# Batch 0's first quarter of q through the hardware DMA queue, and batch 6's softmax sums by matmul

## The chip, the core and the metric

The kernel runs on one core of a Trainium2 chip. The metric is the device time of one launch, in microseconds (us); smaller is better. Engines are named as the profile names them: PE (TensorE, matmuls; PEld its weight loads), DVE (VectorE), ACT (ScalarE), POOL (GpSimd) and SP (SyncE). A DMA that SP issues goes through the hardware queue (q1, `hardware_dynamic`), one that POOL issues through the software queue (q0, `software_dynamic`).

## The reference

A Linformer attention, in which keys and values are projected from 1024 positions to 64 by E and F, and then a feed-forward layer whose hidden layer is the maximum of three projections. There are 8 batches, 8 heads of width 64, and 1024 positions.

```python
def _attn_ref(q, k, v, E, F):
    k_proj = np.einsum('ks,bhsd->bhkd', E, k)
    v_proj = np.einsum('ks,bhsd->bhkd', F, v)
    scale = 1.0 / np.sqrt(q.shape[-1])
    scores = scale * np.matmul(q, k_proj.transpose(0, 1, 3, 2))
    scores = scores - np.max(scores, axis=-1, keepdims=True)
    attn = np.exp(scores)
    attn = attn / (np.sum(attn, axis=-1, keepdims=True) + 1e-09)
    return np.matmul(attn, v_proj).astype(np.float32)

def _moe_ref(x, w1, w2, w3, w_out):
    h = np.maximum(np.maximum(x @ w1, x @ w2), x @ w3)
    return (h @ w_out).astype(np.float32)

# x is the attention's output, as (8192 tokens, 512); w1, w2, w3 are (512, 768), w_out is (768, 512)
```

## The kernel before

The kernel writes its own order for every engine. PE is kept on the feed-forward layer of batch b, and the attention of batch b + 1 is put in between. Inputs are cast to bf16 on their way in by POOL's DMAs; E and F come as fp32 through SP's queue and are cast on DVE and ACT. This is the order of the first loads:

```python
nc.sync.dma_start(out=ef_f[0:KP], in_=E)
nc.sync.dma_start(out=ef_f[KP:P], in_=F)
# load_q, load_kv, load_w: nc.gpsimd.dma_start, fp32 in DRAM to bf16 in SBUF
load_q(LO, slice(0, SPC))        # heads 0 to 3, 4 of 8 rows of each partition: a quarter of q
load_kv(1, LO)                   # k, heads 0 to 3
load_q(HI, slice(0, SPC))
load_kv(1, HI)
load_kv(2, slice(0, 2))          # v, two heads
load_kv(2, slice(2, 4))
# ... identity and constants, weights, the rest of v and q
```

At the start, E and F are turned into `efT`, q's first quarter is turned into `qT`, and k of heads 0 to 3 is projected. The `idle` matmuls compute nothing that is used; they keep PE running.

```python
def turn_ef():
    for i in range(2):
        cols = slice(i * S // 2, (i + 1) * S // 2)
        copy("vs"[i], ef_b[:, cols], ef_f[:, cols])     # fp32 to bf16, on DVE and ACT
    # ... eight 128x128 transposes of ef_b on PE
    for i in range(2):
        copy("vs"[i], efT[:, 4 * i:4 * i + 4, 0:P], ...)

def q_duo(u):                     # per head: 64-wide transposes, 16 of them
    t, ns = bank()
    t = t.bitcast(BF16)
    for gg in range(2):
        heads_q(0, 2 * u + gg, range(SPC), t[:, gg * CHUNK:(gg + 1) * CHUNK])
    o = qTs[0].rearrange("a (g si) p -> a g si p", si=SI)
    copy("v", o[:, 2 * u:2 * u + 2, 0:SPC, :], ...)

def k_duo(u):
    for si in range(SI):
        nc.tensor.matmul(
            out=t[0:KP, 0:4 * D], lhsT=efT[:, si, 0:KP],
            rhs=k_t[:, 4 * u:4 * u + 4, si, :],
            start=(si == 0), stop=(si == SI - 1),
        )
    # ... copied to kp0

idle(3, warm_f)
turn_ef()
q_duo(0)
copy("v", efT[:, :, P:P + KP], efT[:, :, KP:P])
idle(1, warm_f)
k_duo(0)
# ... turn kp0, scores, exponentials, then q_duo(1), k_duo(1), the values of batch 0
```

The first chunk's maxima go through the buffer `hs`, one 512-wide fp32 row for each of six blocks; it is first written at about 25 us.

```python
hs = ffn_sb.tile([P, NJT, CHUNK], FP32, name="hs", bufs=1)
```

There are two ways to get the softmax sums. `zc` lets PE add the exponentials with a matrix of ones and zeros (`pick`, eight matmuls), and ACT inverts the sums. The other way turns the exponentials by a DMA transpose (`turn_p`), adds them on DVE (`sum_p`) and inverts and spreads them from there (`spread_z`). The plan for the loop of batch b, which serves batch n = b + 1, from batch 4 on:

```python
out = {
    (0, 1): [sc(n, 1, now=True), sc(n, 2, now=True), sc(n, 3)],
    (0, 3): [zc(n)],
    (1, 2): [vx(n, 0), vx(n, 1)],
    (1, 6): [vx(n, 2), vx(n, 3)],
}
if n + 1 == B:                    # batch 7: turn_p, sum_p, spread_z in place of zc
    ...
if n + 1 < B:
    out[0, 4] = [qd(n + 1)]
    out[1, 2] = [kvproj(n + 1)] + out[1, 2]
    out[1, 6] += [sc(n + 1, 0)]
if n in (6,):                     # batch 6: the same, with its own places
    del out[0, 3]
    out[0, 4] = [turn_p(n, g) for g in range(NPAIR)]
    # ...
```

Of the kernel before, what the change touches and what calls it, by code (L numbers as in the profile page):

```python
# [15 lines left out]
def kernel(  # L16
# [13 lines left out]
    nc = tc.nc  # L30
# [46 lines left out]
    def two():  # L77
        n = min(range(0, 8, 2), key=lambda n: max(free[n:n + 2]))
        deal((n, n + 1))
        return psum_t[:, n:n + 2, :], (n, n + 1)  # L80
# [20 lines left out]
    def copy(eng, o, i, ns=(), dt=0.65):  # L101
        done = {  # L102
            "v": nc.vector.tensor_copy, "s": nc.scalar.copy, "g": nc.gpsimd.tensor_copy
        }[eng](out=o, in_=i)
        runs(eng, clock["pe"] if ns else 0.0, dt, ns)
        return done
# [49 lines left out]
    def load_q(heads, sis):  # L156
        nc.gpsimd.dma_start(
            out=q_t[:, heads, sis], in_=view(q, 0)[:, heads, sis]
        )
# [4 lines left out]

    LO, HI, ALL = slice(0, H // 2), slice(H // 2, H), slice(0, H)
    V2, V3 = slice(4, 6), slice(6, 8)
    load_q(LO, slice(0, SPC))
    load_kv(1, LO)
    load_q(HI, slice(0, SPC))
    load_kv(1, HI)  # L170
# [122 lines left out]
    def turn_p(b, g):  # L293

        def f():
            if b not in s_T:
                s_T[b] = att.tile([P, NPAIR, 2, SPC, 2], FP32, name="s_T")
            p_T[b, g] = att.tile([P, 2, CHUNK // 2], FP32, name="zi0", bufs=4).rearrange(  # L300
                "p a f -> p (a f)"
            ).bitcast(BF16).rearrange("p (n x) -> p n x", x=P)
            nc.sync.dma_start_transpose(
                out=p_T[b, g], in_=pTs[b, g, 0].rearrange("p h f -> p (h f)")
            )
        return f
# [43 lines left out]
    def vx(b, g):  # L350
        def f():
            scale_x(b, g, 0, SI, values(b, g, 0, SI))
        return f
# [75 lines left out]

    q_pk = {}  # L430

    def pack_q(b, gs, lo, nsi):


        def f():
            if b not in q_pk:
                q_pk[b] = att.tile([P, NPAIR, SI, 2, D], BF16, name="q_p", bufs=1)
            for g in gs:
                copy(
                    "s", q_pk[b][:, g, lo:lo + nsi].rearrange("p si h d -> p h si d"),  # L440
                    qkv[b][0][:, 2 * g:2 * g + 2, lo:lo + nsi], (), 0.58,
                )
        return f

# [184 lines left out]
    def turn_ef():  # L629
        for i in range(2):  # L630
            cols = slice(i * S // 2, (i + 1) * S // 2)
            copy("vs"[i], ef_b[:, cols], ef_f[:, cols])
        t, ns = two()
        t = t.bitcast(BF16)[:, 0]
        src = ef_b.rearrange("k (p si) -> k p si", si=SI)
        for si in range(SI):
            nc.tensor.transpose(
                out=t[:, si * P:(si + 1) * P], in_=src[:, :, si], identity=ident
            )
        pe(0.6)  # L640
        for i in range(2):
            copy(
                "vs"[i], efT[:, 4 * i:4 * i + 4, 0:P],
                t[:, i * CHUNK:(i + 1) * CHUNK].rearrange("p (si x) -> p si x", x=P), ns,
            )
# [46 lines left out]
    def q_duo(u):  # L692
# [5 lines that stand above are left out]
        copy(  # L698
            "v", o[:, 2 * u:2 * u + 2, 0:SPC, :],
            t.rearrange("a (g si p) -> a g si p", si=SPC, p=P), ns, 0.7,  # L700
        )

    C0 = (0, SPC)

    def z(g):
# [5 lines left out]
    idle(3, warm_f)  # L711
    at(6.3)
    turn_ef()
    q_duo(0)
    copy("v", efT[:, :, P:P + KP], efT[:, :, KP:P])
    idle(1, warm_f)
    at(9.0)
# [22 lines left out]
    v_pair(1)  # L740
    at(17.4)

    ffn_sb = ctx.enter_context(tc.tile_pool(name="ffn_sb", bufs=2))
    hTs = {}

    def up_mm(h, i, b, ch, jt, cts, first=0, last=NCT - 1):
# [14 lines left out]
    def up_first(work):  # L761


        def then(key):
            run_later()
            for f in work.get(key, []):
                f()

        hs = ffn_sb.tile([P, NJT, CHUNK], FP32, name="hs", bufs=1)
        hTs[0, 0] = ffn_sb.tile([P, NJT, CHUNK], BF16, name="hT")  # L770
        jts = range(NJT)
        h = {}
        for ct, js in (
            (0, range(0, 4)), (1, range(0, 4)), (0, range(4, 6)), (1, range(4, 6)),
            (2, jts), (3, jts),
        ):
            for jt in js:
                if jt not in h:
                    t, ns = two()
                    for n in (0, 1):  # L780
                        h[jt + n] = t[:, n], ns[n:n + 1]
                up_mm(h[jt][0], 0, 0, 0, jt, (ct,))
                if ct == NCT - 1:
                    copy("sv"[jt % 2], hs[:, jt], *h[jt])
                then((0, ct, jt))
        for i in (1, 2):
            h = []
            for jt in jts:
                h.append(bank())
                up_mm(h[jt][0], i, 0, 0, jt, range(NCT // 2))  # L790
                then((i, "a", jt))
            for jt in jts:
                up_mm(h[jt][0], i, 0, 0, jt, range(NCT // 2, NCT))
                most(hs[:, jt] if i == 1 else hTs[0, 0][:, jt, :], *h[jt], hs[:, jt])
                then((i, jt))
# [93 lines left out]
    def plan(b):  # L889
        n = b + 1  # L890
        if b == 0:
            return {
                (0, 6): [
                    duo[1].sums, duo[1].values, duo[0].scale, duo[1].invert,
                ],
                (0, 7): [
                    qd(1, range(2)), duo[1].scale, qd(1, range(2, 4), "s"), store_now,
                ],
                (1, 1): [kproj(1)],
                (1, 2): [kt(1)],  # L900
                (1, 3): [sc(1, 0, now=True), sc(1, 1), vproj(1), ld(2)],
                (1, 4): [za(1, 0), sc(1, 2, now=True)],
                (1, 5): [za(1, 1)],
                (1, 6): [sc(1, 3, now=True)],
                (1, 7): [za(1, 2)],
                (1, 8): [za(1, 3)],
            }
        if b == 1:
            return {
                (0, 0): [qd(2)],  # L910
                (0, 3): [kproj(2), vproj(2), ld(3, (0,))],
                (0, 4): [kt(2)],
                (0, 5): [sc(2, 0, now=True), sc(2, 1, now=True), sc(2, 2)],
                (0, 6): [sc(2, 3, now=True)],
                (0, 8): [zc(2, nc.gpsimd), ld(3, (1, 2))],
                (1, 1): [qd(3)],
                (1, 3): [vx(2, 0), vx(2, 1)],
                (1, 6): [vx(2, 2), vx(2, 3)],
            }
        if b == 2:  # L920
            return {
                (0, 2): [kproj(3), vproj(3), ld(4)],
                (0, 3): [kt(3)],
                (0, 4): [sc(3, 0, now=True), sc(3, 1)],
                (0, 5): [sc(3, 2, now=True), sc(3, 3, now=True)],
                (0, 7): [zc(3)],
                (0, 8): [qd(4)],
                (1, 3): [kproj(4), vproj(4), ld(5), vx(3, 0), vx(3, 1)],
                (1, 4): [kt(4)],
                (1, 8): [vx(3, 2), vx(3, 3), sc(4, 0)],  # L930
            }
        if n == B:
            return {}
# [6 lines that stand above are left out]
        if n + 1 == B:  # L940
            del out[0, 3]
            out[0, 2] = [turn_p(n, g) for g in range(NPAIR)]
            out[0, 8] = [sum_p(n, 0), sum_p(n, 1)]
            out[0, 9] = [sum_p(n, 2), sum_p(n, 3), spread_z(n)]
            out[1, 5] = out.pop((1, 2))
            out[1, 8] = out.pop((1, 6))
        if n + 1 < B:
            out[0, 4] = [qd(n + 1)]
            out[1, 2] = [kvproj(n + 1)] + out[1, 2]
            out[1, 6] += [sc(n + 1, 0)]  # L950
        if n in (6,):
            del out[0, 3]
            out[0, 4] = [turn_p(n, g) for g in range(NPAIR)]
            out[0, 5] = [qd(n + 1)]
            out[0, 6] = [sum_p(n, 0)]
            out[0, 7] = [sum_p(n, 1)]
            out[0, 8] = [sum_p(n, 2), sum_p(n, 3), spread_z(n)]
            out[1, 2] = [kvproj(n + 1)]
            out[1, 5] = [vx(n, 0), vx(n, 1)]
            out[1, 8] = [vx(n, 2), vx(n, 3), sc(n + 1, 0)]  # L960
            del out[1, 6]
        if n + 2 < B:
            out[1, 3] = [ld(n + 2)]
        return out
# [68 lines left out]
```

## Time and profile before

| what | value |
|---|---|
| time, median of three | 397.53 us (397.27 to 397.54) |
| span of the profiled run | 395.5 us |
| PE busy | 385.6 us, 98% |
| DVE busy | 213.1 us, 54% |
| ACT busy | 149.8 us, 38% |
| E, issue to landing | 3.7 us |
| F, issue to landing | 4.1 us |
| first matmul on k (L655) | starts at 9.90 us |
| eight selection matmuls of `zc` (L264) | 0.61 us from the first to the modelled end of the last |
| one DVE sum of the other way (L310) | 1.21 us |

A line such as `L655 PE MATMUL banks<-k_t,efT` names the source line, the engine, the operation, and what it writes and reads. Times in the timeline are from the start of the span. "Idle before" a group of instructions names what ended the wait. Packets of a DMA queue are counted for all 16 DMA engines together.

### The profile page before, as it was taken

What the parts mean: (1) busy time and instruction counts of PE and PEld (TensorE: products, weight loads), DVE (VectorE), ACT (ScalarE), POOL (GpSimd) and SP (SyncE); (2) the same over time, 40 slices, a digit from 0 to 9 for tenths busy, and PEclk for the clock granted to TensorE, in tenths of its full rate; (3) what the DMA queues carried; (4) which work ended last, traced back from release to release, by engine and by line L of the source; (5) the groups of instructions that cost most, each with busy time, mean ns of one, the idle gap of its engine ahead of it and who ended that gap; (6) DMA issues with size and microseconds to landing.
All of it is one profiled execution on the core that took longest, in us unless ns stands there. A gap on an engine that the chain in (4) does not pass through costs nothing.

```text
span 395.5 us, 5594 instructions
## 1 busy us (share of the span) xinstructions
PE 385.6 (98%) x2181; PEld 173.3 (44%) x2222; DVE 213.1 (54%) x321; ACT 149.8 (38%) x232; POOL 34.4 (9%) x49
## 2 busy tenths in 40 slices
PE   7999999999999999999999999999999999999996
PEld 3544443453445445444444444444444444444443
DVE  2348756751764525655273544744956566655251
ACT  2535638527222562263323532234322623132322
POOL 7440011000400200200002000200000000000000
PEclk9999999999999999999999999999999999999999
DMA  9999999977999999999979969599975425720202
GB/s 147 205 206 207 205 254 142 244 159 160 234 178 257 160 225 201 232 174 201 225 210 140 251 148 250 117 220 187 228 183 160 111 51 163 159 108 0 108 0 106
DMA packets 76250, 68.39 MB, mean 173 GB/s; under 512 B 40448, under 2 KB 68736, under 8 KB 76224
## 3 DMA queue, kind: packets, MB, share of 16 engines
q0 software_dynamic: 29104, 30.41, 48.2%
q1 hardware_dynamic: 46976, 37.56, 38.2%
q8 instruction: 17, 0.28, 0.3%
q10 hardware_dynamic: 144, 0.07, 0.1%
q14 instruction: 9, 0.07, 0.0%
HBM read 69.73 MB, written 16.97 MB: 219 GB/s over the span
## 4 chain that ended last, share of the span: by engine, by line
PE 92%; DVE 2%; DMA 2%; issue 1%; ACT 1%; POOL 0%; DVEq 0%; ACTq 0%; POOLq 0%
PE banks L748 61%; PE banks L856 20%; PE banks L239 2%; DMA k_t<-in_k_dram 2%; PE banks L219 2%; PE banks L412 2%; PE banks L587 1%; DVE xT L375 1%; PE banks L264 1%; ACT zi_all L364 1%; ACT zl L358 1%; PE banks L655 1%; DVE m L817 0%; DVE hT L758 0%; PE banks L626 0%
## 5 line engine op out<-in xcount | busy, mean ns | idle before, releaser
L748 PE MATMUL banks<-xT,w_sb 128*128 128x512 bf16 x1123 | 254.7, 379 | 2.0 <-DVE xT L375 0.3
L748 PEld LDWEIGHTS <-w_sb 128*128 128x128 bf16 x1152 | 110.3, 98 | 136.2 <-issue 7.2
L817 DVE TENSOR_TENSOR m<-banks,h1s 128x512 f32<-128x512 f32 x90 | 62.1, 691 | 117.6 <-ACT h1s L813 71.7
L813 ACT COPY h1s<-banks 128x512 f32<-128x512 f32 x90 | 52.7, 585 | 121.8 <-PE banks L748 121.0
L856 PE MATMUL banks<-wout_sb,hT 128*128 128x512 bf16 x367 | 85.8, 380 | 0.9 <-issue 0.3
L758 DVE TENSOR_TENSOR hT<-banks,m 128x512 bf16<-128x512 f32 x90 | 62.3, 692 | 9.3
L856 PEld LDWEIGHTS <-hT 128*128 128x128 bf16 x378 | 35.2, 98 | 48.4 <-issue 6.9
L102 ACT COPY o_sb<-banks 128x512 f32<-128x512 f32 (+2 forms) x57 | 32.9, 577 | 60.5 <-PE banks L856 57.6
L375 DVE TENSOR_TENSOR xT<-banks,zi_all 128x1024 bf16<-128x1024 f32 x28 | 33.1, 1219 | 14.8 <-PE banks L239 10.2
L230 ACT ACTIVATE pT<-banks 128x1024 bf16<-128x1024 f32 (+1 forms) x32 | 30.2, 975 | 16.0 <-PE banks L219 16.0
L201 POOL DMA_DIRECT2D q_t<-in_q_dram x7 | 6.1, 878 | 197.6 <-DVE m L817 80.9
L102 ACT CAST vp<-banks 64x256 bf16<-64x256 f32 (+1 forms) x11 | 4.7, 424 | 20.5 <-DVE kp L102 11.2
L102 DVE CAST vp<-banks 64x256 bf16<-64x256 f32 (+2 forms) x15 | 6.7, 444 | 9.8 <-ACT vp L102 7.3
L239 PE MATMUL banks<-pT,vp 64*64 64x512 bf16 (+1 forms) x128 | 10.3, 375 | 0.2 <-DVE vp L102 0.2
L102 DVE COPY q_p<-q_t 128x1024 bf16<-128x1024 bf16 x26 | 9.8, 438 | 0.0
L219 PE MATMUL banks<-qT,kpT 64*64 64x512 bf16 (+1 forms) x128 | 9.7, 372 | 0.0
L310 DVE TENSOR_REDUCE s_T<-zi 128x16 f32<-128x1024 bf16 x8 | 9.2, 1210 | 0.0
L102 DVE CAST kp<-banks 128x256 bf16<-128x256 f32 (+2 forms) x9 | 4.6, 509 | 8.5 <-PE banks L587 3.5
L102 DVE COPY o_sb<-banks 128x512 f32<-128x512 f32 (+1 forms) x9 | 5.6, 641 | 5.4 <-PE banks L836 4.5
L358 ACT ACTIVATE zl<-banks 128x512 f32<-128x512 f32 (+1 forms) x8 | 6.5, 810 | 2.9 <-PE banks L239 2.7
L412 PEld LDWEIGHTS <-efT 128*64 128x64 bf16 x128 | 6.6, 110 | 2.1 <-issue 2.1
L626 PE MATMUL banks<-warm_f 128*128 128x512 f32 x8 | 5.7, 852 | 1.5 <-DVE warm_f L175 1.5
(79 smaller groups left out, 140.1 us busy)
## 6 DMA issues: line engine op xcount, KB each, us to landing
out_dram<-o_sb SPq DMA_DIRECT2D x30, 512.0 KB, 3.2
zi_all<-zd SPq DMA_DIRECT2D x20, 512.0 KB, 8.5
q_t<-in_q_dram POOLq DMA_DIRECT2D x7, 1024.0 KB, 10.0
k_t<-in_k_dram POOLq DMA_DIRECT2D x7, 1024.0 KB, 17.1
v_t<-in_v_dram POOLq DMA_DIRECT2D x7, 1024.0 KB, 22.1
zi_all<-zd POOLq DMA_DIRECT2D x4, 512.0 KB, 7.5
w_sb<-in_moe_w_dram POOLq DMA_DIRECT2D x4, 384.0 KB, 10.7
k_t<-in_k_dram POOLq DMA_DIRECT2D x2, 512.0 KB, 8.9
```

The source lines that it names most:

```text
L102: done = {"v": nc.vector.tensor_copy, "s": nc.scalar.copy, "g": nc.gpsimd.tensor_copy}[eng](out=o, in_=i)
L219: nc.tensor.matmul(out=t[c * HALF:(c + 1) * HALF, hp, 0:n * P], lhsT=k_pair(b, g)[rows], rhs=qTs[b][rows, at:at + n, :], start=True, stop= ...
L230: nc.scalar.activation(out=pTs[b, g, lo], in_=t, func=AF.Exp, scale=scale)
L239: nc.tensor.matmul(out=t[hp * HALF:(hp + 1) * HALF, c, 0:nsi * HALF], lhsT=w(rows, hp), rhs=p[rows, hp, :], start=True, stop=True,)
L358: nc.scalar.activation(out=zl, in_=t, func=AF.Ln)
L375: nc.vector.tensor_tensor(out=xTs[b][:, g, lo:lo + nsi, :].rearrange("a (c s) p -> a c (s p)", c=2), in0=t, in1=zi, op=ALU.mult,)
L412: nc.tensor.matmul(out=t[hh * HALF:(hh + 1) * HALF, 0:width], lhsT=efT[:, si, (kv - 1) * KP:kv * KP], rhs=qkv[b][kv][:, heads[hh], si, :], ...
L748: nc.tensor.matmul(out=h, lhsT=w_sb[i][:, ct, jt * P:(jt + 1) * P], rhs=xTs[b][:, ct, ch * SPC:(ch + 1) * SPC, :], start=(ct == first), st ...
L758: nc.vector.tensor_tensor(out=o, in0=h, in1=other, op=ALU.max)
L813: nc.scalar.copy(out=h1s, in_=h[0][0])
L817: nc.vector.tensor_tensor(out=m12, in0=h[1][0], in1=h1s, op=ALU.max)
L856: nc.tensor.matmul(out=o_ps, lhsT=hTs[b, ch][:, jt, tt * P:(tt + 1) * P], rhs=wout_sb[:, jt, :], start=(jt == 0), stop=(jt == NJT - 1),)
```

## The change

The change has two parts, one in place of the other.

The first quarter of q no longer comes through POOL's queue. SP issues it third, after E and F, as fp32, into the first two rows of `hs`, which has to be made earlier for that. DVE and ACT each cast and pack one pair of heads, so that two heads lie side by side, and PE turns eight 128x128 blocks where it turned sixteen 64-wide ones. It is for k to become the first transfer of POOL's queue.

In place of this, batch 6 loses its own plan: its softmax sums come from `zc` as for the batches before it, and only batch 7 keeps the DMA transposes and the sums on DVE.

```diff
-    load_q(LO, slice(0, SPC))
+    ffn_sb = ctx.enter_context(tc.tile_pool(name="ffn_sb", bufs=2))
+    hs = ffn_sb.tile([P, NJT, CHUNK], FP32, name="hs", bufs=1)
+    q_f = hs[:, 0:2].rearrange("p j f -> p (j f)").rearrange(
+        "p (h si d) -> p h si d", h=H // 2, d=D
+    )
+    nc.sync.dma_start(out=q_f, in_=view(q, 0)[:, LO, 0:SPC])
     load_kv(1, LO)
     load_q(HI, slice(0, SPC))
...
-    def pack_q(b, gs, lo, nsi):
+    def pack_q(b, gs, lo, nsi, engs="ss", src=None):
...
-            for g in gs:
+            for g, eng in zip(gs, engs):
+                i = qkv[b][0][:, :, lo:lo + nsi] if src is None else src
                 copy(
-                    "s", q_pk[b][:, g, lo:lo + nsi].rearrange("p si h d -> p h si d"),
-                    qkv[b][0][:, 2 * g:2 * g + 2, lo:lo + nsi], (), 0.58,
+                    eng, q_pk[b][:, g, lo:lo + nsi].rearrange("p si h d -> p h si d"),
+                    i[:, 2 * g:2 * g + 2], (), 0.58,
                 )
...
             copy("vs"[i], ef_b[:, cols], ef_f[:, cols])
+        pack_q(0, (0, 1), 0, SPC, "vs", q_f)()
         t, ns = two()
...
+    def q_first():
+        t, ns = bank()
+        t = t.bitcast(BF16)
+        for gg in range(2):
+            for si in range(SPC):
+                n = gg * SPC + si
+                nc.tensor.transpose(
+                    out=t[:, n * P:(n + 1) * P],
+                    in_=q_pk[0][:, gg, si].rearrange("p h d -> p (h d)"),
+                    identity=ident,
+                )
...
+        copy("v", o[:, 0:2, 0:SPC, :], ...)
...
     turn_ef()
-    q_duo(0)
+    q_first()
     copy("v", efT[:, :, P:P + KP], efT[:, :, KP:P])
...
-        hs = ffn_sb.tile([P, NJT, CHUNK], FP32, name="hs", bufs=1)
...
-        if n in (6,):
-            del out[0, 3]
-            out[0, 4] = [turn_p(n, g) for g in range(NPAIR)]
-            out[0, 5] = [qd(n + 1)]
-            out[0, 6] = [sum_p(n, 0)]
-            out[0, 7] = [sum_p(n, 1)]
-            out[0, 8] = [sum_p(n, 2), sum_p(n, 3), spread_z(n)]
-            out[1, 2] = [kvproj(n + 1)]
-            out[1, 5] = [vx(n, 0), vx(n, 1)]
-            out[1, 8] = [vx(n, 2), vx(n, 3), sc(n + 1, 0)]
-            del out[1, 6]
```

## The prediction

> **What bounds the kernel now.** I read the page's first two parts, then the chain of waits of the first 45 us, then the timeline of the first 28 us, and last the PE timeline of the steady part. The page says that TensorE (PE) is busy everywhere except in the first slice:
>
> ```profile
> PE 385.6 (98%) x2181; PEld 173.3 (44%) x2222; DVE 213.1 (54%) x321; ACT 149.8 (38%) x232; POOL 34.4 (9%) x49
> ...
> PE   7999999999999999999999999999999999999996
> ```
>
> So after the start, the time is the sum of what PE is given, and at the start it is whatever PE waits for. The chain of waits, in order of time, shows that start:
>
> ```profile
> 2.14 7.72 DMA k_t<-in_k_dram
> 9.86 0.04 issue
> 9.90 1.03 PE banks L655 x8
> ```
>
> The first half of k is issued at 2.14 us, behind q's first quarter in the software (POOL) queue, and lands at 9.86 us. From there the chain runs through PE, ScalarE (ACT) and VectorE (DVE) without another DMA in it up to 44 us. What moves the start of the L655 matmuls therefore moves the end by about as much. The timeline shows how much the other inputs of L655 had to spare:
>
> ```profile
> 1.26 0.89 POOL L157 DMA_DIRECT2D q_t<-in_q_dram  x1 [0.81 <-POOLq L1017]
> ...
> 2.14 0.76 POOL L152 DMA_DIRECT2D k_t<-in_k_dram  x1
> ...
> 7.24 0.64 PE L423 MATMUL banks<-ident,q_t 128*64 128x128 bf16 x16
> ...
> 7.92 0.69 DVE L102 COPY qT<-banks 128x1024 bf16<-128x1024 bf16 x1 [0.21 <-PE banks L423]
> 8.53 0.28 DVE L102 COPY efT<-efT 128x512 bf16<-128x512 bf16 x1
> 8.86 0.11 PEld L655 LDWEIGHTS <-efT 128*64 128x64 bf16 x1 [0.76 <-DVE efT L102]
> 9.90 1.03 PE L655 MATMUL banks<-k_t,efT 128*64 128x256 bf16 x8 [0.97 <-DMA k_t<-in_k_dram]
> ```
>
> L655's first weight load is released at 8.86 us by DVE's copy inside efT, which stands in DVE's order behind the copy of the turned q. That path ran 1.0 us ahead of k. It is the path that the change lengthens.
>
> **What the Trainium skill says.** First, "DMA: Bandwidth & Descriptors", section "Queues, rings and completion order": each DMA engine goes round-robin between the queues that have work, a packet at a time. The trace agrees, and shows one packet of each in turn. Between 73.5 and 74.5 us the hardware queue (4 KB stores) and the software queue (1 KB rows of k and v) compete:
>
> ```profile
> q1 hardware_dynamic: 64, 0.26, 68.8%
> q0 software_dynamic: 66, 0.07, 39.6%
> ```
>
> 64 against 66 packets: the columns are packets, MB, and share of the 16 engines. Second, the same page, section "Anatomy of one DMA — SWDGE (gpsimd) path": a wait is released only when the last write is confirmed, well after the last byte. Here F's last hardware packets fall between 4.5 and 5.0 us, and ACT's cast of it starts at 5.57 us, so 0.6 to 1.0 us pass. Third, the same page, section "SWDGE vs HWDGE vs iDMA": only GpSimd's queue casts in flight. That is why q comes as fp32 here and needs two casting copies.
>
> **Part one of the change: batch 6's sums.** For batch 6 the kernel before transposes the exponentials by DMA and adds them on DVE. The changed kernel uses the selection matmuls (line L264) as for batches 4 and 5. Batches as PE sees them begin (first up matmul of a batch, PE timeline) at 168.27, 214.66, 261.04 and 306.85 us. The stretches between these, with the L264 work in each:
>
> ```profile
> 168.27:214.66 46.39, 0.61 (x8) 0.12 (x8) 1.00 1.01 192
> 214.66:261.04 46.38, 0.62 (x8) 0.12 (x8) 1.00 0.93 191
> 261.04:306.85 45.81, 0.00 (x0) 0.00 (x0) 1.00 0.94 194
> ```
>
> Two stretches with the eight L264 matmuls take 46.39 and 46.38 us, the one without takes 45.81. The difference is 0.57 us, and the eight matmuls themselves hold PE for 0.55 us (95.10 to 95.65 us at their first use). The other half of the trade, four DVE sums of 1.21 us each, lies beside PE work (DVE is busy 28.5 of 45.8 us there) and gives nothing back. So part one costs +0.57 us; I see no way for it to be far from this, as the new order is that of the two stretches measured.
>
> **Part two: q's first quarter through the hardware queue.** It takes off POOL one issue of 0.88 us, and k's first half becomes the first software DMA. That does not mean it lands 2 us earlier, because q's bytes use the same 16 engines. The steps:
>
> (a) Where the queues start. Before 4 us only E and F move; between 4.0 and 4.5 us the queues held
>
> ```profile
> q1 hardware_dynamic: 27, 0.07, 64.5%
> q0 software_dynamic: 26, 0.01, 20.2%
> ```
>
> So the first software DMA, issued at 1.26 us, starts moving at about 4.25 us, just as F ends. I expect k to start there in place of q. q, third on the sync queue, is issued at about 2.0 us (E at 0.74, F at 1.38, 0.6 us each) and starts as F ends, at about 4.25 us too.
>
> (b) Packets. q's quarter is 128 x 4 rows of 1 KB, so 32 for each of the 16 engines. k's half is 128 x 4 rows of 2 KB, again 32 for each. Cost of one on an engine: q's cast rows ran 344 packets between 4.5 and 5.5 us, 1.0 x 16 / 344 = 0.047 us each; an fp32 row reads the same 1 KB, so I take 0.047. k's ran 200 packets between 8 and 9 us: 0.080 us each.
>
> (c) Turn by turn, both need 32 x (0.047 + 0.080) = 4.1 us, and end at about 8.3 us. The DMA view of the first 12 us dips to 77 GB/s at 6.0 us and 111 at 6.3, against 171 to 188 around it, where k's first rows came slowly; if they do so again, q uses that hole and ends 0.3 to 0.5 us sooner. With 0.6 to 1.0 us to the release, q lands between 8.5 and 9.2 us, say 8.8, where it now lands before 7.24. k lands about 8.8 instead of 9.86.
>
> (d) From q's landing to L655, by the instruction order of the changed kernel: ACT starts its pack 0.09 us after the landing and takes 0.62 (as the cast of ef_f, 128 x 512, did at 5.57 us); PE turns that half in four 128x128 blocks, 0.37 with the start (eight took 0.65); DVE copies 0.69 to qT and 0.28 inside efT; 0.05 to the weight load. Sum 2.1 us. The pack on DVE (0.45) and the two copies into efT (0.42 and 0.59) lie beside this or just inside it; so does PE's filler L626. The eight transposes saved (0.3 us) lie in a stretch where PE waits.
>
> (e) L655 then starts at 8.8 + 2.1 = 10.9 us, in place of 9.90: +1.0 us. What follows has no DMA wait on PE of its own, and the other loads stay about where they are, so this shift goes to the end.
>
> Sum: 397.53 + 0.57 + 1.0 = 399.1. I put the number a little lower, 398.9, for the rival next.
>
> **Rival one: q lands early and k sets the start.** If a turn of the hardware queue carried several of q's 1 KB rows, or q got its data before the software queue is awake, q would be through by about 6.5 us and land near 7.4. L655 would start at 9.5, and the start gains 0.4 us: 397.53 + 0.57 - 0.4 = 397.7. For it: the order of the copies (the pack ahead of efT) is made for a q that comes just after F, and the first software DMA has a long start-up. Against it: 64 to 66 packets in turn, seen with 4 KB stores, so a turn seems to be one row. I give it about one in four.
>
> **Rival two: the transfer is hidden, k alone sets the start.** k comes 1 us sooner, q lands at 7.7 at the latest, and the start gains a full 0.9 us; against part one's 0.57 that gives 397.2. It needs the engines to carry q beside k for nothing. Against it: the software queue alone already keeps every engine busy (122% of 16 engines between 8 and 9 us). One in twenty.
>
> **Rival three: a new wait in the steady part.** The sync queue loses four DMA transposes, DVE loses four sums, and batch 6 takes the order of batches 4 and 5, which show no stall. I see no wait to add; below one in ten.
>
> **Range and chances.** The steps of part two span from -0.9 us (rival two) to +1.6 us (q lands at 9.4), and part one is firm. That is 397.2 to 399.7, with 0.3 us of spread between runs (397.27 to 397.54). The ends are the less likely, so I take 397.4 to 399.8 for 8 in 10. 2% is 8 us, far outside of anything here, so "within 2%" gets 0.98.
>
> **What would show each step.** Part one: the batch stretch from the fifth batch's first up matmul to the sixth's is 46.4 us, with eight L264 matmuls. (a) and (b): between 5 and 6 us the two queues show like numbers of packets. (c): ACT's pack starts near 8.9 us. (d): L655's first weight load is released by DVE's copy inside efT, not by k. (e): L655 starts near 10.9 us, and the first batch's later steps all stand 1.0 us later. The prediction is wrong if the pack starts before 7.7 us, or if k's landing still releases L655.

## The result, and the profile after

The changed kernel takes 402.38 us (median, 401.89 to 402.93) against 397.50 us: 4.9 us more, a ratio of 1.0124 (95% interval 1.0107 to 1.0142). The prediction said 398.9 us, within 397.4 to 399.8.

The page after, the lines that answer to the two shown of before (each digit is a fortieth of the span, busy share or granted clock in tenths). PE is given about as much as before, in a longer span; what is new is in the first two slices of PE, and in the granted clock, which was 9 throughout:

```profile
PE 387.4 (97%) x2180; PEld 174.0 (43%) x2222; DVE 208.0 (52%) x316; ACT 151.5 (38%) x235; POOL 33.4 (8%) x48
...
PE   5899999999999999999999999999999999999996
...
PEclk9899999999999999999999999999999999999999
```

The chain of waits of the first 45 us names the culprit. Where `k_t` stood, 7.72 us of it, there is now q's hardware transfer into `hs`, issued at 2.01 us and landed at 10.74:

```profile
2.01 8.73 DMA hs<-in_q_dram
10.76 0.44 DVE q_p L102
11.20 0.05 issue
11.25 1.03 PE banks L716 x8
12.28 1.81 PE banks L632 x2
14.09 1.29 PE banks L662 x8
```

The timeline shows who waits. The last bracket of a line is the idle time before it and what ended it:

```profile
10.76 0.62 ACT L102 CAST q_p<-hs 128x512 bf16<-128x512 f32 x1 [4.59 <-DMA hs<-in_q_dram]
10.76 0.43 DVE L102 CAST q_p<-hs 128x512 bf16<-128x512 f32 x1 [4.76 <-DMA hs<-in_q_dram]
11.10 0.42 DVE L102 COPY efT<-banks 128x512 bf16<-128x512 bf16 x1
...
11.25 1.03 PE L716 MATMUL banks<-ident,q_p 128*128 128x128 bf16 x8 [4.30 <-DVE q_p L102]
...
12.07 2.02 PE L632 MATMUL banks<-warm_f 128*128 128x512 f32 x2
...
12.92 0.28 DVE L102 COPY efT<-efT 128x512 bf16<-128x512 bf16 x1
...
14.02 1.36 PE L662 MATMUL banks<-k_t,efT 128*64 128x256 bf16 x8
```

The turned E and F lie ready in PSUM from 6.95 us, but the copies into `efT` stand behind q's pack on DVE and ACT. So PE has nothing to do for 4.3 us, although k has landed at 8.70 us (issued at 1.25, 7.45 us to its landing). Then every PE piece is slow: the filler L632 takes 2.02 us where the same filler, L626, took 1.12 before:

```profile
7.81 1.12 PE L626 MATMUL banks<-warm_f 128*128 128x512 f32 x2
```

The windows view says why; its columns are the stretch, its length, busy time of PE, PEld, DVE, ACT and POOL with the number of instructions, granted clock, DMA share and rate:

```profile
7.00:9.00 2.00, 0.00 (x0) 0.00 (x0) 0.00 (x0) 0.00 (x0) 0.39 (x2) 1.00 1.19 253
9.00:11.25 2.25, 0.00 (x1) 0.01 (x1) 0.49 (x2) 0.49 (x1) 0.70 (x1) 1.00 1.29 229
11.25:14.66 3.41, 3.41 (x13) 1.80 (x14) 1.17 (x3) 0.71 (x2) 1.08 (x2) 0.50 1.24 205
```

For the first 3.4 us after the pause the clock is halved. By the first up matmul of batch 5 (counted from 0) the kernel is 4.44 us behind (265.48 against 261.04 us), and from there to the next batch it takes 46.38 us, 0.57 us more than before, with the eight selection matmuls in it (after the length stand their busy time on PE and PEld, then clock, DMA share and rate):

```profile
265.48:311.86 46.38, 0.62 (x8) 0.12 (x8) 1.00 0.70 161
```

So 4.44 us come from the start and 0.57 from batch 6, together 5.0; the two profiled spans differ by 5.1 us.

### The profile page after: what moved, and what is told of

It reads as the page before. It is cut to its first block, busy times and chain, and to the rows that moved or that the text cites. A ratio compares the mean times of both kernels' runs of the same rounds, so it can differ in the third digit from the quotient of the medians.

```text
span 400.6 us, 5580 instructions
## 1 busy us (share of the span) xinstructions
PE 387.4 (97%) x2180; PEld 174.0 (43%) x2222; DVE 208.0 (52%) x316; ACT 151.5 (38%) x235; POOL 33.4 (8%) x48
## 4 chain that ended last, share of the span: by engine, by line
PE 91%; DVE 3%; DMA 2%; issue 1%; ACT 1%; SPq 0%; DVEq 0%; ACTq 0%
PE banks L772 61%; PE banks L879 19%; PE banks L244 2%; DMA hs<-in_q_dram 2%; PE banks L224 2%; PE banks L417 2%; PE banks L593 1%; DVE xT L380 1%; PE banks L632 1%; PE banks L269 1%; PE banks L662 1%; ACT zi_all L369 1%; ACT zl L363 1%; DVE m L840 0%; DVE hT L782 0%
## 5 line engine op out<-in xcount | busy, mean ns | idle before, releaser
L632 PE MATMUL banks<-warm_f 128*128 128x512 f32 x8 | 6.3, 934 | 1.5 <-DVE warm_f L180 1.5
L206 POOL DMA_DIRECT2D v_t<-in_v_dram x7 | 6.3, 894 | 5.6 <-PE banks L688 3.5
## 6 DMA issues: line engine op xcount, KB each, us to landing
q_t<-in_q_dram POOLq DMA_DIRECT2D x7, 1024.0 KB, 10.5
```

Source lines behind the costliest of these rows:

```text
L206: dma = nc.gpsimd.dma_start(out=tiles[i], in_=view((q, k, v)[i], b))
```

## The experiments

Each "before" is the kernel before, run beside the experiment on the same chip; it had medians of 397.67 to 397.84 us there.

### Each part alone

Batch 6's sums alone, on the kernel before:

```diff
-        if n in (6,):
-            del out[0, 3]
-            out[0, 4] = [turn_p(n, g) for g in range(NPAIR)]
-            ... (the whole block)
```

> The kernel before with only batch 6's sums moved back to the selection matmuls. My theory (the two parts add up, and this one is eight matmuls on a full PE): 0.57 us over before, 398.1 us; the stretch from batch 5's first up matmul to batch 6's is 46.4 us. Rival (the loss of the changed kernel comes from batch 6's new order): about 4.9 us over before, 402.4 us.

Measured: 398.34 us, ratio 1.0016 (1.0008 to 1.0025), so 0.3 to 1.0 us. My theory holds; the rival is out.

q's way alone, with batch 6's plan kept:

```diff
 # the changed kernel
+        if n in (6,):
+            ... (the whole block put back)
```

> The changed kernel with batch 6's own plan put back, so that only q's way in differs from the kernel before. My theory (the start carries the rest): 4.3 us over before, 401.8 us, with q landing at 10.7 us and the first k matmul at 14.0 us as in the changed kernel. Rival (batch 6's order carries it): within 0.6 us of before, 397.5 to 398.1 us.

Measured: 402.11 us, ratio 1.0114 (1.0093 to 1.0136), so 4.5 us over before. q lands at 10.5 us, and the first k matmul starts at 13.57 us. The start carries the loss.

### The half clock

```diff
     turn_ef()
+    idle(4, warm_f)
     q_first()
```

> The changed kernel with four more fp32 filler matmuls between the turn of E and F and the turn of q, 3.4 us of PE work in a stretch where PE stood idle for 4.3 us. Theory that the idle stretch itself brought the half clock (0.5 from 11.25 to 14.66 us): the clock stays 1.00, the turn of q, the filler and the first k matmuls take 0.65, 1.1 and 1.05 us in place of 1.03, 2.0 and 1.36; about 1.5 us less than the changed kernel, 400.9 us. Rival (the half clock has another cause, or the start is bound by q's landing alone): the clock still drops, or the time stays at 402.4 us within 0.3.

Measured: 401.09 us, ratio 1.0087 (1.0072 to 1.0102) against the changed kernel's 1.0124: about 1.5 us less, as expected. The clock stays at 1.00. The PE timeline shows the same pieces at full speed (0.62, 1.08 and 1.06 us):

```profile
12.18 0.62 PE L716 MATMUL banks<-ident,q_p 128*128 128x128 bf16 x8 [1.56 <-DVE q_p L102]
12.64 1.08 PE L632 MATMUL banks<-warm_f 128*128 128x512 f32 x2
13.64 1.06 PE L662 MATMUL banks<-k_t,efT 128*64 128x256 bf16 x8
```

q landed at 11.7 us in this profiled run, 0.9 later than in the changed kernel's, and still the k matmuls start 0.4 us sooner. The pause of 1.56 us left the clock alone; the one of 4.3 us didn't.

### Why q is so late

By head, in four DMAs of 128 rows:

```diff
-    nc.sync.dma_start(out=q_f, in_=view(q, 0)[:, LO, 0:SPC])
+    for h in range(H // 2):
+        nc.sync.dma_start(
+            out=q_f[:, h:h + 1], in_=view(q, 0)[:, h:h + 1, 0:SPC]
+        )
```

> The changed kernel with q's first quarter in four hardware DMAs of one head each (128 rows of 1 KB each, in place of 512 rows in one), in the same place of the queue. Theory rows (the time from a hardware DMA's issue to its first byte grows with its rows: 1.3 us for E's 64 rows, 4.2 us for q's 512, so some 6.5 ns a row): the first head starts as F ends, at about 4.3 us, runs in turn with k, and q lands near 9 us; the time falls by some 1.7 us and more if the clock holds, 399.5 to 400.7 us. Theory behind F (q isn't started until F's landing at 5.5 us is confirmed) and theory software first (k's rows hold q back): q starts at 6.3 us and lands near 10.7 us as before, 402.4 us.

Measured: 403.68 us, ratio 1.0147 (1.0130 to 1.0164). ACT's pack starts at 11.67 us, later still, and q's first row moves at 5.89 us, within what one DMA gave (5.6 to 6.5 us in four traces). The number of rows in a DMA isn't what delays it. The clock is halved here too, and for longer, although PE's two pauses were of 0.89 and 2.05 us only, with 0.69 us of work between them:

```profile
6.70:10.12 3.42, 0.88 (x9) 0.58 (x8) 0.72 (x2) 0.62 (x1) 0.68 (x1) 1.00 1.19 226
10.12:16.94 6.82, 5.21 (x20) 2.56 (x20) 1.86 (x5) 1.10 (x2) 2.36 (x4) 0.50 1.24 208
```

q ahead of E and F in the same queue:

```diff
+    nc.sync.dma_start(out=q_f, in_=view(q, 0)[:, LO, 0:SPC])
     nc.sync.dma_start(out=ef_f[0:KP], in_=E)
     nc.sync.dma_start(out=ef_f[KP:P], in_=F)
-    nc.sync.dma_start(out=q_f, in_=view(q, 0)[:, LO, 0:SPC])
```

> The changed kernel with q's quarter first in the hardware queue, ahead of E and F. Theory rows (512 rows take the queue 4.2 us to begin): q starts at 0.7 + 4.2 = 4.9 us, E and F behind it. Theory behind F (q waits for the transfer ahead of it in its queue): nothing is ahead, q starts at 2.05 us and is through by about 4; so does theory software (a hardware queue whose rows aren't flowing yet when the software queue starts, at about 4.2 us, comes late). Under the last, E and F now meet the software queue: their landing moves from 5.5 to 7 us or later, while q lands near 5; under behind F they land near 7 too. For the time: the first k matmul needs E and F turned, so about 10 to 11 us, 398.5 to 400 us in all.

Measured: 402.78 us, ratio 1.0128 (1.0110 to 1.0146). q moves at once: 353 hardware packets between 2.5 and 3.5 us, 0.045 us each on an engine, and theory rows is out. What is left of E and F at 4.5 us now is what suffers. DMA queues of this kernel from 4.5 to 6.0 us (packets, MB, share of the 16 engines):

```profile
q0 software_dynamic: 160, 0.16, 70.5%
q1 hardware_dynamic: 27, 0.07, 19.1%
```

and from 6.5 to 8.0 us:

```profile
q0 software_dynamic: 139, 0.14, 78.0%
q1 hardware_dynamic: 62, 0.21, 40.2%
```

The hardware queue stands nearly still just after the software queue's start, and then comes back. E's rows had been moving since 3.5 us, so it was the queue that already flowed that stood still. E and F are cast at 9.74 us only, and the clock is halved as well, from 8.57 to 15.40 us:

```profile
8.57:15.40 6.83, 4.98 (x25) 3.27 (x26) 2.12 (x5) 1.73 (x3) 1.48 (x3) 0.50 1.26 199
```

The first k matmul starts at 14.09 us in place of 10 to 11, and the time is 2.8 us above the range I gave. Theory behind F doesn't explain the pause; it came with the software queue's start.

q in ACT's hardware queue:

```diff
-    nc.sync.dma_start(out=q_f, in_=view(q, 0)[:, LO, 0:SPC])
+    nc.scalar.dma_start(out=q_f, in_=view(q, 0)[:, LO, 0:SPC])
```

> The changed kernel with q's quarter issued by ACT at its very start, in a hardware queue of its own beside E and F. Theory behind F: q has nothing ahead of it, starts near 2.05 us and lands near 5.5 us. Theory software: the same, as q's rows flow before the software queue starts. Theory rows: q starts near 4.9 us and lands near 9 us. If q is early, k sets the start: k lands near 8 us, the first k matmul starts at 8.3 to 9.0 us with a full clock, and the time is 0.6 us of batch 6 less about 1.2, 396.9 us (within 396.5 to 397.6), against 397.8 for the kernel before on this chip.

Measured: 399.35 us, ratio 1.0044 (1.0026 to 1.0063): better than the changed kernel, and 1.8 us over before, where I had expected a gain. q is early, as expected, but E and F, issued at the same moment, now wait for q: their rows start at 3.6 us in place of 2.1, they are cast at 7.88 us in place of 5.57, and the first k matmul starts at 10.54 us. The newcomer waits here too, and here both queues are hardware queues. The 16 executions spread from 397.98 to 401.92 us: the eight with a mean clock of 0.998 or more took 397.98 to 399.09, the eight with 0.991 to 0.996 took 399.61 to 401.92. The trace is of one of the former, with a pause of 1.61 us on PE; that the others lost their clock at the start as well is likely but not shown. Where the clock held, the loss is 0.2 to 1.3 us, batch 6's included.

The software queue later:

```diff
     nc.sync.dma_start(out=q_f, in_=view(q, 0)[:, LO, 0:SPC])
+    nc.gpsimd.memset(wout_sb[:, 0:4], 0.0)
     load_kv(1, LO)
```

> The changed kernel with a fill of a part of the output weights' buffer on POOL ahead of its first DMA, some 2.7 us, so that the software queue (and with it k and the identity) comes later. It computes the same. Theory software (q's rows come late because k's rows already flow): q now starts behind F, at about 4.3 us or sooner, and is through before k starts at about 7. Theory behind F (q waits until F has landed, at 5.5 us) and theory rows (4.2 us after issue): q starts at 6.3 us as before. The time of the whole will be longer, as k lands near 10.5 us; what is read is q's start.

Measured: 399.12 us (one run). q now follows F at once. The queues from 5 to 6 us, where the changed kernel had 184 software packets and not one of the hardware queue:

```profile
q1 hardware_dynamic: 279, 0.28, 99.4%
q0 software_dynamic: 18, 0.02, 10.8%
```

Holding k back by 1.2 us makes the whole some 3 us faster than the changed kernel; by the run with PE kept busy, about 1.5 us of that is the clock, which held here. That is what theory software says, and the other two theories don't. Some tens of q's rows were left when the software queue got going, and they made the landing late again (pack at 9.10 us).

Short rows ahead:

```diff
-    load_kv(1, LO)
     load_q(HI, slice(0, SPC))
+    load_kv(1, LO)
```

> The changed kernel with q's second quarter (1 KB rows, 0.047 us each on an engine) ahead of k's first half (2 KB rows, 0.080 us each) in the software queue. In the changed kernel q's hardware transfer began to move at 6.4 us, 2.1 to 2.5 us after the software queue. Theory rows ahead (the newcomer waits for the rows that the other queue has already handed to the engines, some 25 to 32 for each): 25 to 32 x 0.047 = 1.2 to 1.5 us after the software queue's start, so it starts at 5.3 to 5.8 us. Rival (a fixed time of 2 us, whatever the rows): 6.2 us or later.

Measured: 403.35 us (one run). By the packet records, q's first row moves at 5.3 us, and a tenth of its rows has moved by 5.64 us, half by 6.55 us; in the changed kernel it was 6.4, 7.13 and 8.48 us. The queues between 5 and 7 us in this run:

```profile
q0 software_dynamic: 359, 0.19, 72.1%
q1 hardware_dynamic: 333, 0.34, 50.3%
```

and in the changed kernel:

```profile
q0 software_dynamic: 318, 0.33, 106.2%
q1 hardware_dynamic: 37, 0.04, 6.8%
```

The first row alone can't decide, as it spreads: in four traces with the changed kernel's transfers (changed kernel, q only, PE kept busy, q turned last) it moves at 5.6 to 6.5 us. Later rows do: in those four a tenth has moved by 6.84 to 7.40 us, half by 8.30 to 8.83 us. By the time a tenth of q's rows has moved, 386 software packets have gone in this run, in 1.7 us, and 407 to 455 in the four others, in 2.7 to 3.9 us. So with shorter rows in front the pause is shorter by about as much as the rows are, as theory rows ahead says; a fixed time doesn't fit. q lands no sooner for it (pack at 11.06 us), since its last rows then take turns with k's long ones, and the k matmuls get late too. It is one run, the packets are counts over all engines, and 32 rows for an engine are the whole first transfer of the software queue: whether q waits for a number of rows or for that transfer isn't separated.

### What the order of the engines adds

q packed and turned after k's projection and turn:

```diff
-        pack_q(0, (0, 1), 0, SPC, "vs", q_f)()
...
     turn_ef()
-    q_first()
     copy("v", efT[:, :, P:P + KP], efT[:, :, KP:P])
     idle(1, warm_f)
     k_duo(0)
     idle(2)
     kt_duo(0)
+    pack_q(0, (0, 1), 0, SPC, "vs", q_f)()
+    q_first()
```

> The changed kernel with q packed and turned only after k's projection and turn, so that E, F and k don't wait for q on any engine. Theory (the loss of the start is q's landing passed on by the engines' order, and the half clock that comes of the idle PE): k's first matmul starts near 9.0 us, the clock stays full, the scores start near 12.6 us in place of 16.4, and the time is 3.7 us below the changed kernel: 398.7 us, or 1.0 to 1.2 us over before. Rival (the order isn't the cause; the shared engines make k late as well): the first k matmul starts no sooner than 11 us, and the time stays over 400.5 us.

Measured: 399.14 us, ratio 1.0038 (1.0024 to 1.0051). The transfer is as late as ever (pack at 11.19 us), but only the turn of q waits for it, and PE doesn't stand long enough to lose its clock:

```profile
9.15 1.03 PE L661 MATMUL banks<-k_t,efT 128*64 128x256 bf16 x8 [0.74 <-DMA k_t<-in_k_dram]
10.12 0.61 PE L632 MATMUL banks<-warm 128*128 128x512 bf16 x2
10.70 0.23 PE L674 MATMUL banks<-ident,kp 64*128 64x64 bf16 x2
11.68 0.62 PE L715 MATMUL banks<-ident,q_p 128*128 128x128 bf16 x8 [0.75 <-DVE q_p L102]
```

That takes back about 3.4 us of the 4.9. Of the 1.5 us that stay, 0.57 are batch 6's, and the rest is the scores' start at 13.08 us in place of 11.99.

### Is k first worth anything?

k ahead of q in the software queue of the kernel before, with nothing new in the hardware queue:

```diff
-    load_q(LO, slice(0, SPC))
     load_kv(1, LO)
+    load_q(LO, slice(0, SPC))
...
-    q_duo(0)
...
     k_duo(0)
-    idle(2)
+    q_duo(0)
     kt_duo(0)
```

> The kernel before with k's first half ahead of q's first quarter in the software queue, nothing in the hardware queue but E and F, and q turned between k's projection and the turn of k (in place of two fillers). It tries what the change was for, k first, without sharing the engines. Theory that k, and not the sum of k and q, sets the start: k lands near 7.5 us, q near 9.7, the first scores matmul at about 11.4 us in place of 11.99, and the time falls by 0.6 us to 397.2 on this chip. Rival (the scores need both, so their sum sets the start, whatever the order): within 0.2 us of the kernel before.

Measured: 397.81 us, ratio 1.0001 (0.9990 to 1.0011). The scores start at 11.28 us, 0.7 sooner, and nothing is left of it at the end. PE's waits between 9 and 25 us show where it went:

```profile
PE banks L681 <- DMA v_t<-in_v_dram: 1.0, 1, 1.0
PE banks L219 <- DVE kpT L102: 0.4, 1, 0.4
```

The matmuls on v's third pair, L681, now wait 1.0 us for their data; in the trace of the kernel before they didn't, though their weight load stood 0.34 us for it. Part of the 1.0 us is v's own lateness: the pair landed at 20.66 us here against 19.91. That landing spreads from run to run (20.57 in the run with batch 6's sums alone, whose start is the same as before's), for a reason that isn't shown. But at 19.91 it would have taken the gain as well, since before the weight load was held until 19.95 us. The start is bound by k, but by v right behind it.

Then F in ACT's queue, alone and with k first:

```diff
-    nc.sync.dma_start(out=ef_f[KP:P], in_=F)
+    nc.scalar.dma_start(out=ef_f[KP:P], in_=F)
```

> The kernel before with F issued by ACT at its start, in a hardware queue of its own, so that E (which fills partitions 0 to 63) and F (64 to 127) are issued at the same time. In the runs so far E's and F's 4 KB rows took 0.25 to 0.3 us each on an engine, and the software queue's first row moved only when F's last had. Theory that two queues overlap the halves: E and F are through by about 3.5 us in place of 4.4, the software queue starts about 0.7 us sooner, k lands near 9.1 us, and with it all loads; the time falls by 0.5 to 0.8 us against before. Rival (the engines serve E's rows and then F's at the same rate, or the software queue's start is set by its own issue): within 0.2 us of before.

> The same with k's first half ahead of q's first quarter in the software queue, as in the run with k ahead of q, which had its scores 0.7 us sooner and then stood 0.9 us waiting for v. Theory that the sum of all loads up to v's third pair sets the start there: it gains what the run with F on ACT's queue gains and no more (within 0.3 us of it). Rival (k's order is worth its 0.7 us again once loads come sooner): 0.5 us or more below that run.

Measured: 397.65 us, ratio 1.0001 (0.9992 to 1.0010), and 397.66 us, ratio 0.9997 (0.9989 to 1.0005). The two queues don't overlap: between 2 and 3 us only ACT's queue moves (39 packets of F), E's rows follow from 3.2 us, and both are through at about 4.2 us against 4.4. With k first, the scores start at 11.05 us, and the wait for v is back:

```profile
20.30 0.62 PE L681 MATMUL banks<-v_t,efT 128*128 128x128 bf16 x8 [0.82 <-DMA v_t<-in_v_dram]
```

None of the versions tried beats the kernel before.

## Why the prediction was wrong, point by point

- **Part one, +0.57 us: right.** The stretch takes 46.38 us (46.4 said), and the part alone costs 0.3 to 1.0 us (0.5 by the medians).
- **(a) "I expect k to start there in place of q ... q ... starts as F ends, at about 4.25 us too": right for k, wrong for q. This is the step that failed.** k's rows move from about 4 us. q's don't move before 6.4 us, although F's last had gone by 4.7. I had the round-robin between queues from a stretch in which both were already flowing, and took it to hold from a newcomer's first row. The runs show that a newcomer waits first: q behind k (the changed kernel, from about 4.25 to 6.4 us) and E and F behind q. With the software queue held back q starts at once, and with shorter rows ahead a tenth of it has moved 1.2 to 1.8 us sooner. That q is late because the software queue was ahead of it is shown; how many rows go first is not, and with q ahead of E the wait held with only some ten software packets for an engine (160 in all) gone by.
- **(b) and (c), "Turn by turn, both need ... 4.1 us": about right as a size, once the turns begin.** From 6.4 us to q's last row at 10.35 us it is 3.95 us, and between 7 and 9 us the queues show 302 and 307 packets. The prediction's "one packet of each in turn" is more than such counts show: a turn may be one row or several. The landing, said to be 8.8 us, was 10.74. That is 1.9 us: the start was 2.15 us late, and the release after the last row took some 0.35 us, not the 0.6 to 1.0 taken from F. k landed at 8.70 us, near the 8.8 said, but partly by luck: it had the engines to itself for 2 us and shared them only for its last third. (Of the 200 packets that (b) counted as k's, 185 were its rows, so a row of k cost 0.086 rather than 0.080 us.)
- **(d) "Sum 2.1 us" from landing to L655: the order on DVE was right, the size was not.** It took 3.3 us. The pieces were counted at full clock, and after 4.3 us of empty PE it was halved. The turn of q took 1.03 us in place of 0.65, and the filler, which (d) put beside the path, took 2.02 us and ended at 14.09, 0.9 us behind DVE's copy inside `efT` (12.92 + 0.28): the filler set the start, and not that copy. I never asked how long PE's wait would be and what comes after it. With PE kept busy it takes 1.95 us from q's pack to k's first matmul.
- **(e) "+1.0 us": 4.12 us at L662's start.** 1.0 said, 1.9 from the landing, 1.2 from the clock; and 0.3 us more inside L662, still at half clock, makes the 4.4 us by which the scores start late (16.44 in place of 11.99) and which go on to the end.
- **Rivals.** I gave early q one chance in four. By the run with k first it would have gained next to nothing: there PE waited at v's third pair, and the end didn't move. An early q with E, F and k on time was in no run. "What moves the start of the L655 matmuls therefore moves the end by about as much" held upwards and, in the runs with k first, not downwards. The trace of before had a hint of it, a weight load of L681 held 0.34 us by v at 19.95 us. No new wait came in the steady part.
- **The round-robin.** The Trainium skill, "DMA: Bandwidth & Descriptors", section "Queues, rings and completion order", has each DMA engine go round-robin between the queues it has work for. The trace agrees with that once both queues flow (302 to 307 packets from 7 to 9 us), and not in the first 2 us of the later one (318 to 37 from 5 to 7 us).

What stays open: what holds a newcomer's rows back inside the engines. The packet records carry no engine, so rows ahead on one engine can't be counted, and all that is said of the wait rests on starts and on counts over all 16.

## What to carry to other kernels

A transfer moved to another queue doesn't start beside the one that already flows: ask what was given to the engines ahead of it, and which instructions stand behind it in an engine's own order. Before you count the pieces behind a late landing, count the pause on PE: after the 4 us pauses of these runs the pieces ran at half clock, and once after 2 us. And before paying for an earlier start, look for the next landing in the chain's shadow, as it caps the gain.

## What the hardware showed beyond expectation

- A pause of 4.1 to 4.3 us on PE was followed by a clock of 0.50: for 3.4 us in the changed kernel and with q alone, for 6.8 us with q ahead of E and with short rows ahead (filler 2.02 us in place of 1.08 to 1.12). Pauses of 1.0 us (before), 1.56 us (PE kept busy) and 1.8 us (software later) were not. The length of one pause alone doesn't decide: with q by head the clock fell at 10.12 us, 1.65 us into a pause, when PE had been busy for 0.88 of the 3.42 us before.
- A transfer that came while another queue flowed moved nothing for 1.3 to 3.0 us (q after the software queue's first row, in five traces). It was so for hardware behind hardware (E behind q: first row at 3.6 us, q's at 2.0), and for software behind hardware (with q in ACT's queue, POOL's first row moved at 5.6 us in place of about 4). With q ahead of E it was the hardware queue, flowing already, that nearly stopped when the software queue started (27 packets against 160 from 4.5 to 6.0 us), so the order in which the queues arrive isn't the whole of it.
- Two hardware queues in place of one left the rate of E and F as it was: through at about 4.2 us against 4.4.
